# A transformer block on one core: the VectorE share of the softmax exponential as two summed terms instead of six, with more of it on VectorE and K projected without a trip through DRAM

## The chip, the cores and the metric

One of the eight cores of a Trainium2 chip runs the whole kernel. The core has five engines that work at the same time and wait for each other by semaphores: TensorE (PE: matmuls, and PEld: its weight loads), VectorE (DVE), ScalarE (ACT), GpSimd (POOL) and SyncE (SP), which here issues nearly all DMA transfers. Matmuls write to PSUM, eight banks of 512 fp32 values on each of 128 partitions; the other engines read them from there. SBUF is the large on-chip memory, DRAM is outside the core.

The metric is the device time of one execution in microseconds (us), the median of several runs. A profile is one further execution; its span is a little shorter than the device time.

## What is computed

A block with adaptive layer norm: attention with 32 heads of 20 dimensions over 2048 tokens, then a gated feed-forward part. Cut to what matters:

```python
# A_x [1, 2048, 640], A_wqkv [640, 1920], A_wo [640, 640]
# B_w_gate, B_w_up [640, 1536], B_w_down [1536, 640], c [1, 640], w_mod [640, 3840]
mod = (silu(c) @ w_mod).reshape(1, 6, 1, 640)
sa, ca, ga, sb, cb, gb = mod[:, 0], ..., mod[:, 5]

h = layernorm(x) * (1 + ca) + sa
q, k, v = split_heads(h @ wqkv)                  # 32 heads, Dh = 20
scores = einsum('bhqd,bhkd->bhqk', q, k) * Dh ** -0.5
p = softmax(scores)                              # 32 x 2048 x 2048 exponentials
x = x + ga * (merge_heads(einsum('bhqk,bhkd->bhqd', p, v)) @ wo)

h = layernorm(x) * (1 + cb) + sb
x = x + gb * (((h @ w_gate) * (h @ w_up)) @ w_down)   # B_x is not used
```

The exponentials are the largest elementwise part: 134 million of them.

## The kernel before

The program is written by a small scheduler in Python. Tasks carry an engine, a rough duration, a priority and dependencies; the scheduler runs them through a model of the engines once, and the order that comes out on each engine is what the chip executes. [...]

**Chunks, items, units, quads.** Queries are cut into five chunks. A chunk has eight items (four heads each), and an item is cut into units: one unit is a 128 x 512 tile of scores of one head. A unit goes either to ScalarE or, in fours called quads, to VectorE. `QUADS` says how many quads each item of each chunk has.

```python
CHUNKS = [(0, 512), (512, 512), (1024, 512), (1536, 256), (1792, 256)]
QUADS = [(1, 2, 2, 3, 2, 3, 2, 3), 3, 3, (1, 1, 2, 1, 1, 1, 1, 1), (1, 1, 1, 1, 1, 0, 0, 0)]
SHIFTS = (0, 18, 34, 56, 77, 105)
NB0, NSS = 3, 2        # buffers for VectorE's first and for its further terms
NPS = 4                # slots of exponentials, in each of two rings
K_DIRECT = (0, 1)
```

**Exponential on ScalarE** (L1214): groups of three and two units by turns, from PSUM to bf16 in SBUF.

```python
        def fexp(e, nu=nu, b0=b0, cellp=cellp, g=g):
            return e.activation(PPs[g % 2][:, cellp["p"], 0:nu * 512],
                                ps[:, b0:b0 + nu, :].rearrange("p b c -> p (b c)"), AFT.Exp, scale=ESCALE)
```

**Exponential on VectorE.** Q is scaled so that a score, plus a bias, written as a 16-bit integer is the bit pattern of a bf16 number near the exponential: the upper bits are the exponent, the lower seven a straight line in place of 2^f. This is one instruction a unit (L1238). To bend the straight lines to the curve, five more copies of the quad are made with other offsets (L1252), and all six terms are summed.

```python
            def fp1(e, st_=st_, x=x, cell=cell):
                return e.tensor_scalar(DB0[:, st_["slot"], x * 512:(x + 1) * 512], bank(cell["b"]), EBIAS, 0.0,
                                       op0=ALU.add, op1=ALU.max)
        ...
        for jj in range(1, NSH):
            def fsh(e, st_=st_, cell=cell, jj=jj):
                return e.tensor_scalar(DSS[:, cell["s"], :], DB0[:, st_["slot"], :], float(SHIFTS[jj]), None, op0=ALU.add)
            tsx = Task("dve", 575.0, fsh, list(st_["p1"]), prio=2.5 + .001 * qi,
                       name=f"SH.{qi}.{jj}")
            tsx.acq = [(sSS, "s", 1)]
```

**The sum costs no instruction of VectorE**: TensorE multiplies every term with V and accumulates in PSUM. A VectorE unit thus has six value matmuls where a ScalarE unit has one (L1596, four heads side by side, 32 columns of the array each). V carries a column of ones, so the softmax denominator comes out of the same sums.

```python
            ems.append(lambda e, i=i, kt=kt, stt=stt, stp=stp: e.matmul(
                ps[32 * s:32 * s + mc, BPV, 0:u.n],
                Vf[:, (kt * H + 4 * u.j + s) * VW:(kt * H + 4 * u.j + s) * VW + mc],
                srcf()[:, i * u.n:(i + 1) * u.n], tile_position=(0, 32 * s), start=stt, stop=stp,
                skip_group_check=True))
```

After an item's last value matmul VectorE transposes, divides and transposes back (L1305 to L1313). Items go through one PSUM bank, one after the other.

**Projections.** A score matmul reads K and Q of a head at partitions 32 s. `kq_round` ("direct", L862) projects four heads of 20 columns to 32-row places. `packed_round` (L914) projects 128 columns with no gaps, in fewer rounds, and the rows go to DRAM scratch and come back to their places:

```python
        # packed_round, K
        pcs = [(0, w, lambda: KS[656 * tc + r0:656 * tc + r0 + w, :])]
        ...
        kt_ready[(j, tc)] = [dma("sp", 32 * 1024, lambda e, j=j, s=s: e.dma_start(
            KT[32 * s:32 * s + 32, j, tc * 512:(tc + 1) * 512],
            KS[656 * tc + 80 * j + DH * s:656 * tc + 80 * j + DH * s + 32, :]),
            dps, prio=1.4, dur=450.0) for s in range(4)]
```

Here K of the first item's heads comes directly in the first two token blocks, Q of the first two items in the first block; all else is packed. An eviction of a projection (`evac`) can be taken over by ScalarE early in the kernel.

**The feed-forward part** of a chunk (`suffix`) is spread by gates over the next chunk's exponentials; that of the last chunk stands alone at the end.

The softmax here doesn't subtract the row's maximum and nothing guards it: scores larger than these inputs give would overflow.

## Time and profile before

| | |
|---|---|
| device time, median of 3 runs | 869.92 us (869.12 to 872.37) |
| span of the profile | 865.9 us |
| ScalarE, exponentials (L1214) | 691 instructions, 788.3 us busy |
| TensorE, scores (L1180) | 2560 matmuls, 295.2 us busy |
| TensorE, values with ScalarE's units (L1596, PP) | 2184 matmuls, 171.9 us busy |
| TensorE, values with VectorE's terms (L1596, DSS and DB) | 2256 matmuls, 183.8 us busy |
| VectorE, first term (L1238) | 320 instructions, 217.2 us busy |
| VectorE, shifted terms (L1252) | 400 instructions, 265.9 us busy |
| transposes of an item's sums (L1305) | first 63.2 us, last 830.4 us |

"Busy" is the time in which at least one instruction of the group runs on its engine; the mean of one instruction can be longer than the step from one to the next, since neighbours overlap. A line such as `L1214` is the line of the kernel that wrote the instruction, `out<-in` names the tiles. Where the profile says `<-PE ps_all L1180 9.7`, the engine was idle for 9.7 us before instructions of that group until that line of PE released them.

### The profile page before, as it was taken

To read this page: it belongs to the slowest core of one execution; us is meant where nothing else is said; L and a number is where in the kernel's file an instruction comes from. 1 tells how busy PE (TensorE), PEld (TensorE's weight loads), DVE (VectorE), ACT (ScalarE), POOL (GpSimd) and SP (SyncE) were. 2 spreads that over 40 slices of the span, in tenths; PEclk is the share of its full clock that TensorE was granted. 3 is DMA by queue.
4 is the path that set the end of the run, shared out by engine and by line. 5 is a ranking of instruction groups with operands and counts; after the bars stand their busy time and mean duration, and the time that the engine had idled before them with its cause. 6 is when DMAs were issued, how large, how long until landed. Compare 5 with 4: busy or idle time off the path is not lost.

```text
span 865.9 us, 30616 instructions
## 1 busy us (share of the span) xinstructions
PE 829.4 (96%) x13568; PEld 327.5 (38%) x13568; DVE 713.1 (82%) x1338; ACT 802.5 (93%) x718; POOL 32.0 (4%) x65
## 2 busy tenths in 40 slices
PE   8899999999999999999999999999999999999998
PEld 4433333322233322233333322223445444455577
DVE  7865888796999999999889999999779877775463
ACT  4698999999999999899999999999999999999931
POOL 2300000000001000000000100000001100000000
PEclk9997999999999999999999999999999999999999
DMA  9163331122510125110301011110310036203640
GB/s 300 38 216 94 92 86 37 29 71 76 156 29 23 33 55 146 43 24 6 66 10 44 5 36 44 44 36 2 67 50 7 21 75 139 59 21 82 136 88 18
DMA packets 118459, 56.37 MB, mean 65 GB/s; under 512 B 84439, under 2 KB 118327, under 8 KB 118327
## 3 DMA queue, kind: packets, MB, share of 16 engines
q1 hardware_dynamic: 117399, 53.26, 24.2%
q8 instruction: 107, 1.75, 0.9%
q10 hardware_dynamic: 928, 1.15, 0.4%
q14 instruction: 25, 0.20, 0.1%
HBM read 42.93 MB, written 9.16 MB: 60 GB/s over the span
## 4 chain that ended last, share of the span: by engine, by line
PE 44%; ACT 34%; DVE 15%; issue 3%; DMA 2%; POOL 1%; SPq 1%; DVEq 0%; ACTq 0%
ACT PP L1214 34%; PE ps_all L747 16%; PE ps_all L1596 13%; PE ps_all L1180 12%; DVE DB L1238 4%; DVE DSS L1252 3%; PE ps_all L914 2%; DVE st L802 1%; DMA k_rows<-KPA 1%; DVE st L1400 1%; DVE xck L1390 1%; DVE OT L1305 1%; DVE xn L1407 1%; PE ps_all L829 1%; DMA stg<-in_B_w_gate_dram 1%
## 5 line engine op out<-in xcount | busy, mean ns | idle before, releaser
L1214 ACT ACTIVATE PP<-ps_all 128x1536 bf16<-128x1536 f32 (+1 forms) x691 | 788.3, 1279 | 13.5 <-PE ps_all L1180 9.7
L1180 PE MATMUL ps_all<-QT,KT 32*128 32x512 bf16 (+1 forms) x2560 | 295.2, 341 | 14.5 <-ACT PP L1214 11.5
L1252 DVE TENSOR_SCALAR DSS<-DB 128x2048 int16<-128x2048 int16 x400 | 265.9, 683 | 20.0 <-PE ps_all L1596 17.7
L1238 DVE TENSOR_SCALAR DB<-ps_all 128x512 int16<-128x512 f32 x320 | 217.2, 682 | 38.7 <-PE ps_all L1180 37.0
L1180 PEld LDWEIGHTS ps_all<-QT,KT 32*128 32x128 bf16 x2560 | 77.2, 91 | 256.6 <-ACT PP L1214 185.7
L1596 PE MATMUL ps_all<-PP,Vf 128*32 128x512 bf16 (+3 forms) x2184 | 171.9, 344 | 1.5 <-DVE OT L1305 1.5
L1596 PE MATMUL ps_all<-DSS,Vf 128*32 128x512 bf16 (+2 forms) x1880 | 151.7, 351 | 0.0
L747 PE MATMUL ps_all<-h2T,stg 128*32 128x512 bf16 x1440 | 109.7, 381 | 2.8 <-DVE DB L1238 1.7
L1596 PEld LDWEIGHTS ps_all<-PP,Vf 128*32 128x32 bf16 (+1 forms) x2184 | 48.3, 94 | 95.3 <-issue 84.9
L1596 PEld LDWEIGHTS ps_all<-DSS,Vf 128*32 128x32 bf16 (+1 forms) x1880 | 47.8, 96 | 36.1 <-issue 16.0
L747 PE MATMUL ps_all<-wd,hprod 128*32 128x320 bf16 x1152 | 55.2, 300 | 0.4 <-DVE DB L1238 0.3
L747 PEld LDWEIGHTS ps_all<-h2T,stg 128*32 128x32 bf16 x1440 | 34.8, 96 | 35.1 <-issue 9.4
L1465 DVE CAST gsb<-ps_all 128x512 bf16<-128x512 f32 (+1 forms) x48 | 29.5, 615 | 10.8 <-PE ps_all L747 10.6
L747 PEld LDWEIGHTS ps_all<-wd,hprod 128*32 128x32 bf16 x1152 | 29.2, 96 | 14.9 <-issue 4.8
L747 PE MATMUL ps_all<-wV,hT 128*32 128x320 bf16 x640 | 32.9, 300 | 1.9 <-DVE DB L1238 0.8
L1403 POOL TENSOR_SCALAR sd<-mv 128x1 f32<-128x1 f32 x14 | 7.0, 499 | 739.7 <-DVE mv L1402 739.7
L747 PE MATMUL ps_all<-wo,Ocp 128*32 128x320 bf16 x640 | 31.9, 300 | 0.4 <-DVE xck L1390 0.3
L1596 PE MATMUL ps_all<-DB,Vf 128*32 128x512 bf16 (+2 forms) x376 | 32.1, 349 | 0.0
L1305 DVE STREAM_TRANSPOSE OT<-ps_all 128x512 f32<-128x512 f32 (+1 forms) x40 | 24.2, 605 | 8.8 <-PE ps_all L1596 8.6
L914 PE MATMUL ps_all<-hT,wk 128*32 128x512 bf16 x380 | 29.9, 381 | 0.4 <-DVE Vf L994 0.4
L914 PE MATMUL ps_all<-hT,wq 128*32 128x512 bf16 x375 | 29.0, 394 | 0.9 <-DVE Vf L994 0.3
L1476 DVE TENSOR_TENSOR hprod<-ps_all,gsb 128x512 bf16<-128x512 f32 x36 | 24.5, 681 | 5.3 <-PE ps_all L747 5.3
(107 smaller groups left out, 486.6 us busy)
## 6 DMA issues: line engine op xcount, KB each, us to landing
stg<-in_B_w_gate_dram SPq DMA_DIRECT2D x50, 160.0 KB
stg<-in_B_w_up_dram SPq DMA_DIRECT2D x50, 160.0 KB
KT<-k_rows SPq DMA_DIRECT2D x120, 32.0 KB
QT<-q_rows SPq DMA_DIRECT2D x22, 128.0 KB
wm<-in_w_mod_dram SPq DMA_DIRECT2D x3, 800.0 KB
k_rows<-KPA SPq DMA_DIRECT2D x18, 128.0 KB
x<-in_A_x_dram SPq DMA_DIRECT2D x7, 320.0 KB
xck<-in_A_x_dram SPq DMA_DIRECT2D x3, 640.0 KB
```

The lines of the kernel that those rows point to most:

```text
L747: return lambda e, b: e.matmul(ps[32 * x:32 * x + 32, b, 0:n], lhs()[:, 32 * x:32 * x + 32], rhs(), tile_position=(0, 32 * x), start=st, s ...
L802: bns.append(dve(393, lambda e, t=t, i=i, hf=hf: e.bn_stats(st[:, i, 6 * hf:6 * hf + 6], x0[:, t, 320 * hf:320 * hf + 320]), [d_x[tc][i // ...
L829: f = lambda e, b, i=i, k=k: e.transpose(bankh(b)[:, i * 128:(i + 1) * 128], xn[:, s2, i, k * 128:(k + 1) * 128], ident[:])
L914: f = [lambda e, b_, k=k, x=x: e.matmul(ps[x:x + min(32, w - x), b_, :], wx[:, k, r0 + x:r0 + min(x + 32, w)], hT[tc][:, k, :], tile_posit ...
L1180: ems.append(lambda e, i=i, kt=kt: e.matmul(dstf()[:, i * u.n:(i + 1) * u.n], KT[32 * u.s:32 * u.s + 32, u.j, kt * 128:(kt + 1) * 128], QT ...
L1214: return e.activation(PPs[g % 2][:, cellp["p"], 0:nu * 512], ps[:, b0:b0 + nu, :].rearrange("p b c -> p (b c)"), AFT.Exp, scale=ESCALE)
L1238: return e.tensor_scalar(DB0[:, st_["slot"], x * 512:(x + 1) * 512], bank(cell["b"]), EBIAS, 0.0, op0=ALU.add, op1=ALU.max)
L1252: return e.tensor_scalar(DSS[:, cell["s"], :], DB0[:, st_["slot"], :], float(SHIFTS[jj]), None, op0=ALU.add)
L1305: t1 = Task("dve", n * 1.1 + 70, lambda e: e.transpose(OT[:, 0:n], ps[:, BPV, 0:n]), [], prio=0.0, name=f"T1.{it}")
L1465: f = lambda e: e.tensor_copy(gsb[:, gs, 0:n], ps[:, r.b["b"], 0:n])
L1476: f = lambda e: e.tensor_tensor(hprod[:, fc, 0:n], ps[:, r.b["b"], 0:n], gsb[:, gs, 0:n], ALU.mult)
L1596: ems.append(lambda e, i=i, kt=kt, stt=stt, stp=stp: e.matmul(ps[32 * s:32 * s + mc, BPV, 0:u.n], Vf[:, (kt * H + 4 * u.j + s) * VW:(kt * ...
```

## The change

On VectorE the exponential becomes a parabola in the mantissa. Read the 16-bit pattern as 2^e (1+f). Masking out the mantissa and setting the exponent of one half gives (1+f)/2; its product with the pattern itself is 2^e (1+f)^2 / 2. The second term is the pattern with the mantissa cleared but for one bit, 2^e (1 + 2/128). Their sum, 2^e ((1+f)^2 / 2 + 1.016), is close to 1.5 times 2^(e+f), and the constant factor goes into the bias. So a quad has two terms in place of six, made by three instructions in place of five: mask and exponent in the form of the shift, and one product of two tensors. The value matmuls of a VectorE unit fall from six to two. What is freed is used to move more units from ScalarE: 92 quads in place of 80.

K of all heads and Q of the first token block are projected directly. K never goes to DRAM; more projection rounds are run for it.

Further constants of the scheduler (leads, gates, priorities) are set anew.

```diff
-QUADS = [(1, 2, 2, 3, 2, 3, 2, 3), 3, 3, (1, 1, 2, 1, 1, 1, 1, 1), (1, 1, 1, 1, 1, 0, 0, 0)]
-SHIFTS = (0, 18, 34, 56, 77, 105)
-D_LEAD = 0.35
-NB0, NSS = 3, 2
+QUADS = [(3, 2, 3, 3, 3, 3, 4, 3), 3, (3, 3, 3, 3, 3, 3, 4, 3), (1, 2, 1, 2, 1, 2, 0, 2), 1]
+D_LEAD = 0.377
+NB0, NSS = 2, 3
 NPS = 4
+TS_4X, TT_2X = 600.0, 1145.0
 ... (gates, leads)
-K_DIRECT = (0, 1)
-K_LEAD = 0.4
+K_DIRECT = (0, 1, 2, 3)
+Q_DIRECT = 8
+K_ALL = (0, 1, 2, 3)
+KD_LEAD = 0.593
 ...
-SHIFT_GAIN = 3.046480226123085
+QUAD_GAIN = 0.597233983857778
+NTERM = 2
 ...
-    late.append((.95, 2560, lambda p, g: kq_round("Q", 1, 0, p, g)))
-    for b in range(4):
+    for j in range(1, Q_DIRECT):
+        late.append((j - .05, 2560, lambda p, g, j=j: kq_round("Q", j, 0, p, g)))
+    for b in range(4 if Q_DIRECT < NSET else 0):
 ...
     for tc in range(4):
-        for b in range(nblk(tc)):
+        for j in range(1, NSET if tc in K_ALL else 0):
+            late.append((j + tc / 4 - KD_LEAD, 2560, lambda p, g, j=j, tc=tc: kq_round("K", j, tc, p, g)))
+        for b in range(0 if tc in K_ALL else nblk(tc)):
 ...
-        for jj in range(1, NSH):
-            def fsh(e, st_=st_, cell=cell, jj=jj):
-                return e.tensor_scalar(DSS[:, cell["s"], :], DB0[:, st_["slot"], :], float(SHIFTS[jj]), None, op0=ALU.add)
+        def fm(e, st_=st_):
+            return e.tensor_scalar(DSS[:, st_["ss"][0], :], DB0[:, st_["slot"], :], 0x7F, 0x3F00, op0=ALU.bitwise_and,
+                                   op1=ALU.bitwise_or)
+
+        def fx(e, st_=st_):
+            d = DSS[:, st_["ss"][0], :].bitcast(BF16)
+            return e.tensor_tensor(d, DB0[:, st_["slot"], :].bitcast(BF16), d, ALU.mult)
+
+        def fe(e, st_=st_):
+            return e.tensor_scalar(DSS[:, st_["ss"][1], :], DB0[:, st_["slot"], :], 0x7F80, 2, op0=ALU.bitwise_and,
+                                   op1=ALU.bitwise_or)
+        tm = term(fm, list(st_["p1"]), TS_4X, "M", slot=0)
+        term(fx, [tm], TT_2X, "X", src=0, last=True)
+        term(fe, list(st_["p1"]), TS_4X, "EX", slot=1, src=1, last=True)
```

## The prediction

> **What bounds the kernel now.** I read the page's busy line first, then ScalarE's timeline and waits, then a table by stage, then the groups by shape, then a few microseconds of VectorE and TensorE. The busy line:

> ```profile
> PE 829.4 (96%) x13568; PEld 327.5 (38%) x13568; DVE 713.1 (82%) x1338; ACT 802.5 (93%) x718; POOL 32.0 (4%) x65
> ```

> Two engines look full. Which one sets the end is told by who waits for whom. ScalarE's timeline shows its first exponential at 17.28 us and the last one ending at 829.00 us, and between long runs without a gap:

> ```profile
> 339.73 25.32 ACT L1214 ACTIVATE PP<-ps_all 128x1536 bf16<-128x1536 f32 x22
> 367.41 2.37 ACT L1214 ACTIVATE PP<-ps_all 128x1536 bf16<-128x1536 f32 x2 [2.36 <-PE ps_all L1596]
> 370.11 50.57 ACT L1214 ACTIVATE PP<-ps_all 128x1536 bf16<-128x1536 f32 x44 [0.34 <-PE ps_all L1180]
> ```

> The columns are start, length, instruction, count and, in brackets, the idle time before. 44 ACTIVATEs (22 pairs of three and two units; a unit is one 512-wide score tile) take 50.57 us: 2.30 us for five units, 0.46 us a unit. In the view of waits ScalarE waits for TensorE only briefly, while TensorE's weight loads wait mostly for ScalarE to free score banks:

> ```profile
> PEld ps_all L1180 <- ACT PP L1214: 185.7, 471, 1.4
> ...
> ACT PP L1214 <- PE ps_all L1180: 9.7, 14, 2.6
> ```

> The table by stage (I cut at the first exponential, 120 us, the four chunk changes and the last exponential; columns are window, its length, busy time and count of PE, PEld, DVE, ACT, POOL, granted clock, DMA share, GB/s):

> ```profile
> 17.30:120.00 102.70, 95.78 (x1408) 36.09 (x1404) 75.10 (x157) 88.70 (x81) 9.79 (x22) 0.95 0.42 115
> 120.00:238.00 118.00, 113.94 (x1500) 34.94 (x1492) 98.31 (x166) 117.90 (x105) 0.00 (x0) 1.00 0.27 74
> 238.00:429.00 191.00, 185.37 (x2499) 59.58 (x2491) 181.79 (x319) 187.70 (x166) 5.09 (x8) 1.00 0.20 48
> 429.00:620.00 191.00, 185.34 (x2541) 60.05 (x2542) 178.09 (x310) 190.22 (x168) 4.38 (x8) 1.00 0.13 32
> 620.00:724.00 104.00, 99.57 (x2138) 48.66 (x2130) 84.69 (x164) 103.51 (x92) 5.93 (x8) 1.00 0.18 45
> 724.00:829.00 105.00, 103.08 (x2334) 54.05 (x2330) 64.61 (x132) 104.89 (x92) 1.58 (x4) 1.00 0.41 89
> 829.00:866.00 37.00, 32.60 (x1020) 27.27 (x1020) 17.54 (x45) 4.47 (x12) 1.23 (x2) 1.00 0.12 33
> ```

> ScalarE's busy time from 17.3 to 829 us sums to 792.9 of 811.7 us, so it idles 18.8 us, of which 14.0 us lie before 120 us and 3.3 us in the second chunk. So three pieces make the span: 17.3 us until the first exponential, 811.7 us of ScalarE with little idle, 37 us of last gated block. In the middle only fewer ScalarE units, or less of those 18.8 us, can shorten it. VectorE is at 95% and 93% in the third and fourth windows: it is what keeps more units from moving to it.

> [...]

> ```profile
> L1252 DVE TENSOR_SCALAR DSS<-DB 128x2048 int16<-128x2048 int16 x400 | 265.9, 683 | 20.0 <-PE ps_all L1596 17.7
> L1238 DVE TENSOR_SCALAR DB<-ps_all 128x512 int16<-128x512 f32 x320 | 217.2, 682 | 38.7 <-PE ps_all L1180 37.0
> L1162 DVE TENSOR_TENSOR wo<-wo,gab 128x640 bf16<-128x640 bf16 x5 | 2.3, 467 | 0.0
> L1310 DVE TENSOR_TENSOR OTn<-OT,invT 128x512 bf16<-128x512 f32 x24 | 16.4, 682 | 0.2
> ```

> [...] 640 bf16 elements take less time (467 ns) than 512 with an fp32 input (682 ns). No run yet shows 2048 in tensor_tensor. [...] no trace here has an AND/OR. [...]

> **Part by part.** One full instruction behind another starts 0.60 us later on VectorE (timeline, starts 281.08, 281.68, 282.28 us):

> ```profile
> 281.08 0.68 DVE L1238 TENSOR_SCALAR DB<-ps_all 128x512 int16<-128x512 f32 x1
> 281.68 0.68 DVE L1252 TENSOR_SCALAR DSS<-DB 128x2048 int16<-128x2048 int16 x1
> 282.28 0.69 DVE L1238 TENSOR_SCALAR DB<-ps_all 128x512 int16<-128x512 f32 x1
> ```

> and four concurrent 512-wide value matmuls start 0.22 us after the four before them (482.56 and 482.78 us):

> ```profile
> 482.56 0.39 PE L1596 MATMUL ps_all<-DB,Vf 128*32 128x512 bf16 x4
> 482.78 0.39 PE L1596 MATMUL ps_all<-DSS,Vf 128*32 128x512 bf16 x4
> ```

> Units: 3 x 8 x 64 + 2 x 8 x 32 = 2048. A quad moves four to VectorE. Before 2048 - 320 = 1728 on ScalarE, after 2048 - 368 = 1680, so 48 fewer. At 0.46 us that is **-22.1 us** on the bounding engine (chunk by chunk 24, 0, 4, 8 and 12 units: -11.0, 0, -1.8, -3.7, -5.5).

> VectorE, per quad: before 4 reads of PSUM + 5 shifts = 9 x 0.60 = 5.40 us, 80 quads 432 us. After 4 reads + mask + exponent = 6 x 0.60, [...] The order of instructions shows 49 projection evictions on it after, 38 before (+6.6 us), and three layer-norm evictions fewer (about 0.5 us each). In all about +10 us: flat. But it shifts: in the second chunk 24 quads fall from 129.6 to 113.8 us, so its 95% falls to about 87%. In the first chunk 18 quads (97 us) become 24 (114 us), and with the evictions 173 us of 221 us (first two windows) become some 195 us of about 210 us, 93%. Full, not over.

> TensorE: the summed terms go from 6 x 320 = 1920 to 2 x 368 = 736 unit matmuls, by fours 480 to 184 times 0.22 us, -65 us; ScalarE's units -48, -2.6 us. Projections of Q and K go from 835 to 1100 matmuls, +265, +66 fours, +14.6 us. Net -53 us, in an engine that ScalarE makes wait: no direct gain. Scores are unchanged at 2560 matmuls.

> ScalarE also takes evictions in the head: by the order, hT 9 instead of 6 (0.78 us each), KT 4 instead of 2 and KPA 0 instead of 1 (0.59 us each): **+2.9 us**, partly inside idle time.

> DRAM scratch: 24 writes of K rows and 120 reads into KT go, and the packed rounds of the first Q. The chain of waits has such a transfer from 50.5 to 68 us, but ScalarE runs 13 ACTIVATEs from 50.13 to 65.17 us: hidden there. What it may give is a part of the 14.0 us idle before 120 us. On the other side stand the extra projection rounds, in a stretch where PE is busy 93%. I take **-5 us** of idle in all (an estimate, from 18.8 us present), of which the second chunk's 3.3 us are the easiest.

> First exponential: the same three projections and the same transposes go ahead of it, 0. End: the last item has a quad now and had none, so its last value matmuls may wait for VectorE: **+1 us**, a guess; the 37 us themselves run the same matmuls.

> Sum: 865.9 - 22.1 + 2.9 - 5 + 1 = 842.7 us of span. The device time before is 869.92 us for a span of 865.9 us, 4.0 us more: about 846 us.

> **Rivals.** (a) ScalarE has no idle time left after the change: 17.3 + 336 x 2.30 + 7.6 (head evictions) + 37 + 4.0 gives 839 us. For it: TensorE has 53 us less to do. Against it: the early idle time comes from transposes and projections that must be done first. (b) VectorE becomes the bound in the first chunk: at 93% by my count, value matmuls of a quad then come late, the eight slots of exponentials fill and ScalarE stops. Were the load 5% over full, ScalarE would lose about 10 us of the 210: 853 to 857 us. (c) [...] Slower by far; only the missing measurement of a bit operation speaks for it. (d) PE had been the true limit and 53 us come off: below 825 us; the gapless ScalarE rows speak against it.

> **Range and chances.** The floor of (a) and the middle of (b) bound the range, 838 to 857 us. 2% faster is 852.5 us, above the sum by 6 us; it takes most of (b) to miss it. Faster 0.81, same 0.15; slower, nearly (c) alone, 0.04.

> **What would show it.** Right: 672 ACTIVATEs of exponentials still at 2.30 us a pair, in runs of 20 and more; mask and exponent near 683 ns[...]; ScalarE idle between first and last exponential under 18 us; PE busy well below 96%; the tail near 37 us. Wrong: ScalarE waiting for scores that wait for VectorE's quads before 230 us, a bit operation of 2 us or more, a first exponential later than 18 us, or a tail of 40 us.

## The result and the profile after

The changed kernel takes **857.71 us** (853.04 to 857.92, 4 executions) beside 869.99 us: ratio 0.9848, 95% interval 0.9819 to 0.9877. Measured again later, six executions beside their own runs of the kernel before: 851.4 us, ratio 0.9821 (0.9787 to 0.9855). It is faster by 1.5 to 1.8%; 846 us had been predicted, in a range of 838 to 857 us: the first median lies 0.7 us above that range, the second inside it. A ratio is always the time over that of the kernel before, measured beside it.

The page of the changed kernel, its busy line and four groups (count, then busy us and mean ns of one):

```profile
PE 798.6 (93%) x12393; PEld 308.9 (36%) x12393; DVE 718.1 (84%) x1270; ACT 780.8 (91%) x703; POOL 31.2 (4%) x65
...
L1220 ACT ACTIVATE PP<-ps_all 128x1536 bf16<-128x1536 f32 (+1 forms) x672 | 763.8, 1319 | 23.6 <-PE ps_all L1186 22.9
...
L1277 DVE TENSOR_TENSOR DSS<-DB,DSS 128x2048 bf16<-128x2048 bf16 x92 | 111.1, 1208 | 0.1
...
L1272 DVE TENSOR_SCALAR DSS<-DB 128x2048 int16<-128x2048 int16 x92 | 62.5, 679 | 1.3
L1280 DVE TENSOR_SCALAR DSS<-DB 128x2048 int16<-128x2048 int16 x92 | 62.7, 681 | 1.0 <-PE ps_all L1616 1.0
```

The work is what it was meant to be: 672 exponentials on ScalarE, the product at 1208 ns, mask and exponent at 680 ns, as fast as the shifts they replace (683 ns). ScalarE's timeline shows where the gain leaks (start, length, count, idle before and what ended it):

```profile
41.43 5.57 ACT L1220 ACTIVATE PP<-ps_all 128x1024 bf16<-128x1024 f32 x5 [3.63 <-PE ps_all L1186]
49.73 3.07 ACT L838 ACTIVATE hT<-ps_all,mcol 128x512 bf16<-128x512 bf16 x4 [2.73 <-PE ps_all L832]
59.44 103.54 ACT L1220 ACTIVATE PP<-ps_all 128x1536 bf16<-128x1536 f32 x91 [6.64 <-PE ps_all L1186]
166.93 37.31 ACT L1220 ACTIVATE PP<-ps_all 128x1024 bf16<-128x1024 f32 x33 [3.95 <-PE ps_all L1186]
...
221.12 367.01 ACT L1220 ACTIVATE PP<-ps_all 128x1536 bf16<-128x1536 f32 x324 [1.65 <-PE ps_all L1186]
...
785.77 34.22 ACT L1220 ACTIVATE PP<-ps_all 128x1536 bf16<-128x1536 f32 x30 [1.59 <-PE ps_all L1186]
```

In the middle 324 ACTIVATEs run without a gap, 162 pairs at 2.266 us. The longest such row of the kernel before is this:

```profile
89.66 197.77 ACT L1214 ACTIVATE PP<-ps_all 128x1536 bf16<-128x1536 f32 x174 [1.48 <-PE ps_all L1180]
```

That is 87 pairs at 2.273 us, nearly the same pace. The prediction's 2.30 us came in part from reading a shorter row: a row's length counts its last ACTIVATE in full and the others only from start to start, and neighbours overlap (the two of a pair take 1.49 and 1.07 us in the mean of the kernel before, 2.56 us together). Ahead of the rows of L1220 shown above ScalarE waits for scores. The view of waits:

```profile
PEld ps_all L1186 <- ACT PP L1220: 198.5, 495, 1.2
...
ACT PP L1220 <- PE ps_all L1186: 22.9, 15, 6.6
```

TensorE's weight loads still mostly wait for ScalarE, but ScalarE's waits for scores are 22.9 us where they were 9.7 us. Three windows of the table by stage:

```profile
17.30:120.00 102.70, 95.60 (x1371) 36.59 (x1368) 85.99 (x167) 84.97 (x80) 10.10 (x23) 0.97 0.26 70
120.00:230.00 110.00, 104.20 (x1338) 33.08 (x1339) 96.14 (x152) 103.06 (x91) 0.00 (x0) 0.97 0.06 17
230.00:420.00 190.00, 178.44 (x2326) 56.51 (x2322) 174.86 (x286) 189.95 (x169) 5.01 (x8) 1.00 0.26 67
```

In the first two windows VectorE (third pair of columns) is at 182 of 212.7 us, 86%, and not the bound. ScalarE (fourth) idles 17.7 us in the first and 6.9 us in the second, where the first two windows of the kernel before had 14.0 and 0.1 us.

The span as a sum along ScalarE, from its timeline (idle: the gaps between its rows, first to last exponential); the last column is a later profile of the same changed kernel, used below:

| us | before | changed | changed, again |
|---|---|---|---|
| until the first exponential | 17.3 | 17.9 | 17.6 |
| exponentials | 789.7 | 764.5 | 764.3 |
| other ScalarE work between | 4.7 | 7.7 | 7.5 |
| idle between | 17.3 | 29.9 | 24.4 |
| after the last exponential | 36.9 | 35.8 | 35.8 |
| span | 865.9 | 855.8 | 849.5 |

25.2 us of exponentials are saved and 12.6 us come back as idle time, with 3.0 us of added evictions. The question for the experiments was what makes the 12.6 us.

### The profile page after: what moved, and what is told of

It is laid out like the page before. It is cut to its first block, busy times and chain, and to the rows that moved or that the text cites. A ratio compares the mean times of both kernels' runs of the same rounds, so it can differ in the third digit from the quotient of the medians. Undisturbed runs are those within 1.5% of the kernel's fastest.

```text
span 855.8 us, 28189 instructions
## 1 busy us (share of the span) xinstructions
PE 798.6 (93%) x12393; PEld 308.9 (36%) x12393; DVE 718.1 (84%) x1270; ACT 780.8 (91%) x703; POOL 31.2 (4%) x65
## 3 DMA queue, kind: packets, MB, share of 16 engines
q1 hardware_dynamic: 106998, 45.14, 21.2%
## 4 chain that ended last, share of the span: by engine, by line
ACT 41%; PE 35%; issue 12%; DVE 11%; POOL 0%; ACTq 0%; DVEq 0%
ACT PP L1220 41%; PE ps_all L750 13%; PE ps_all L1186 10%; PE ps_all L1616 7%; DVE DB L1244 3%; PE ps_all L865 2%; DVE st L805 1%; PE ps_all L917 1%; DVE DSS L1272 1%; DVE DSS L1277 1%; DVE OT L1325 1%; DVE hT L840 0%; DVE xn L816 0%; DVE OTn L1330 0%; DVE OcT L1333 0%
## 5 line engine op out<-in xcount | busy, mean ns | idle before, releaser
L1220 ACT ACTIVATE PP<-ps_all 128x1536 bf16<-128x1536 f32 (+1 forms) x672 | 763.8, 1319 | 23.6 <-PE ps_all L1186 22.9
L1186 PE MATMUL ps_all<-QT,KT 32*128 32x512 bf16 (+1 forms) x2560 | 310.6, 342 | 31.8 <-ACT PP L1220 24.3
L1244 DVE TENSOR_SCALAR DB<-ps_all 128x512 int16<-128x512 f32 x368 | 247.3, 682 | 60.2 <-PE ps_all L1186 59.2
L1186 PEld LDWEIGHTS ps_all<-QT,KT 32*128 32x128 bf16 x2560 | 81.5, 91 | 269.8 <-ACT PP L1220 198.5
L1616 PE MATMUL ps_all<-PP,Vf 128*32 128x512 bf16 (+1 forms) x2116 | 167.8, 345 | 0.2
L1277 DVE TENSOR_TENSOR DSS<-DB,DSS 128x2048 bf16<-128x2048 bf16 x92 | 111.1, 1208 | 0.1
L1616 PEld LDWEIGHTS ps_all<-PP,Vf 128*32 128x32 bf16 (+1 forms) x2116 | 47.8, 94 | 91.8 <-issue 83.2
L1616 PE MATMUL ps_all<-DSS,Vf 128*32 128x512 bf16 (+2 forms) x888 | 76.2, 353 | 0.2
L1272 DVE TENSOR_SCALAR DSS<-DB 128x2048 int16<-128x2048 int16 x92 | 62.5, 679 | 1.3
L1280 DVE TENSOR_SCALAR DSS<-DB 128x2048 int16<-128x2048 int16 x92 | 62.7, 681 | 1.0 <-PE ps_all L1616 1.0
L865 PE MATMUL ps_all<-hT,wk 128*32 128x512 bf16 x640 | 46.8, 386 | 2.3 <-ACT hT L838 0.9
L1325 DVE STREAM_TRANSPOSE OT<-ps_all 128x512 f32<-128x512 f32 (+1 forms) x40 | 24.1, 604 | 10.2 <-PE ps_all L1616 10.1
L1616 PEld LDWEIGHTS ps_all<-DSS,Vf 128*32 128x32 bf16 (+1 forms) x888 | 23.8, 96 | 19.7 <-issue 7.6
```

The source lines that it names most:

```text
L865: f = [lambda e, b, k=k, s=s: e.matmul(ps[32 * s:32 * s + 32, b, :], wx[:, k, w0 + DH * s:w0 + DH * s + 32], hT[tc][:, k, :], tile_positio ...
L1186: ems.append(lambda e, i=i, kt=kt: e.matmul(dstf()[:, i * u.n:(i + 1) * u.n], KT[32 * u.s:32 * u.s + 32, u.j, kt * 128:(kt + 1) * 128], QT ...
L1220: return e.activation(PPs[g % 2][:, cellp["p"], 0:nu * 512], ps[:, b0:b0 + nu, :].rearrange("p b c -> p (b c)"), AFT.Exp, scale=ESCALE)
L1272: return e.tensor_scalar(DSS[:, st_["ss"][0], :], DB0[:, st_["slot"], :], 0x7F, 0x3F00, op0=ALU.bitwise_and, op1=ALU.bitwise_or)
L1277: return e.tensor_tensor(d, DB0[:, st_["slot"], :].bitcast(BF16), d, ALU.mult)
L1280: return e.tensor_scalar(DSS[:, st_["ss"][1], :], DB0[:, st_["slot"], :], 0x7F80, 2, op0=ALU.bitwise_and, op1=ALU.bitwise_or)
```

## The experiments

Candidates: the three quads in the first item; the direct projections; TensorE's granted clock, which the trace shows at 0.5 in more places than before; or the claim itself that ScalarE sets the end. This table gathers what the runs' traces show; the idle columns are ScalarE's gaps in us by stretch of the span, "half" is the time at granted clock 0.5 between about 22 us and the end:

| run | time, us | to 70 | 70-120 | 120-240 | 240-725 | later | half, us |
|---|---|---|---|---|---|---|---|
| before | 869.99 | 8.3 | 5.4 | 0 | 3.7 | 0 | 10.2 |
| changed | 857.71 | 17.4 | 0 | 6.9 | 1.9 | 3.7 | 27.3 |
| terms only | 873.39 | 8.0 | 15.8 | 0 | 0.2 | 0.8 | 27.3 |
| direct only | 876.96 | 7.5 | 0.9 | 8.2 | 1.7 | 0.4 | 3.4 |
| K through DRAM | 860.38 | 15.0 | 10.0 | 0 | 11.7 | 0.5 | 61.4 |
| clock held up | 863.17 | 18.9 | 0 | 8.7 | 3.6 | 1.2 | 6.8 |
| item 0, one quad | 848.32 | 10.2 | 1.0 | 4.5 | 3.3 | 0.3 | 6.8 |
| Q earlier | 859.67 | 17.7 | 0 | 3.1 | 6.7 | 2.9 | 44.4 |
| direct, set again | 845.98 | 7.2 | 0 | 4.7 | 4.0 | 0 | 17.1 |
| DRAM, set again | 848.16 | 8.3 | 5.7 | 2.4 | 5.0 | 0.7 | 23.9 |
| same 92 quads | 861.24 | 10.2 | 1.4 | 11.9 | 4.5 | 1.1 | 23.9 |
| quads later | 857.08 | 13.2 | 8.0 | 6.8 | 1.9 | 0.5 | 20.5 |
| changed, again | 851.4 | 17.9 | 0 | 4.0 | 1.9 | 0.5 | 10.2 |

One caution holds for all but two of them: every new constant lets the scheduler write a new order everywhere, so a time carries all its side effects. The stretches are read with more trust than the sums.

**The terms alone.** The new exponential with the old quads, the old paths of K and Q and the old leads and gates (but two first buffers and three others, as in the change).

```diff
-QUADS = [(3, 2, 3, 3, 3, 3, 4, 3), 3, (3, 3, 3, 3, 3, 3, 4, 3), (1, 2, 1, 2, 1, 2, 0, 2), 1]
-K_DIRECT, Q_DIRECT, K_ALL = (0, 1, 2, 3), 8, (0, 1, 2, 3)
+QUADS = [(1, 2, 2, 3, 2, 3, 2, 3), 3, 3, (1, 1, 2, 1, 1, 1, 1, 1), (1, 1, 1, 1, 1, 0, 0, 0)]
+K_DIRECT, Q_DIRECT, K_ALL = (0, 1), 2, ()
 (leads, gates and caps as before the change)
```

> Only the new exponential (two terms, three VectorE instructions a quad) with the 80 quads of before, K packed through DRAM and all leads and gates of before. Theory (ScalarE sets the end; TensorE and VectorE work only matter through the waits they cause): 1728 units stay on ScalarE, so its exponentials stay near 785 us, the idle time between first and last exponential near 19 us, and the time near 866 us (ratio 0.99 to 1.00), although TensorE loses some 70 us and VectorE some 50 us of work. Rival (TensorE at 96% was a bound of its own): the time falls with TensorE's work, to 850 us or less.

873.39 us, ratio 1.0029 (1.0007 to 1.0051): not faster at all. VectorE's busy time falls from 713.1 to 659.6 us and 1386 matmuls are gone, and none of it reaches the end, because ScalarE's exponentials take 787.5 us as before. That TensorE bounds the kernel is out. The loss against the expected 866 us is mostly one wait, in ScalarE's timeline of this run:

```profile
85.80 2.36 ACT L1220 ACTIVATE PP<-ps_all 128x1536 bf16<-128x1536 f32 x2 [0.32 <-PE ps_all L1186]
98.01 2.37 ACT L1220 ACTIVATE PP<-ps_all 128x1536 bf16<-128x1536 f32 x2 [9.84 <-PE ps_all L1186]
```

The scores at the end of that wait stood waiting for Q, which in this run still comes back from DRAM for most heads (TensorE's timeline):

```profile
97.56 0.70 PE L1186 MATMUL ps_all<-QT,KT 32*128 32x512 bf16 x7 [3.95 <-DMA QT<-q_rows]
```

The page's clock row shows a dent in slices 4 and 5 of its 40 (the two lower digits), which lie between about 65 and 109 us:

```profile
PEclk9997799999999999999999999999999999999999
```

The two halved stretches in it are 74.1 to 84.3 and 98.0 to 108.2 us. During the wait itself the clock is at 1.00, as a window over it shows (clock third from the end):

```profile
88.20:98.00 9.80, 5.68 (x45) 2.12 (x36) 1.91 (x5) 0.00 (x0) 0.00 (x0) 1.00 0.50 119
```

So the late Q makes this wait, and not the clock.

**The direct projections alone**, in the kernel before (80 quads, six terms; the hunks of `K_ALL` and `Q_DIRECT` applied, `KD_LEAD = 0.593`).

> Only the projection part: six terms and 80 quads as before, but K of all heads and Q of the first block direct, constants of before otherwise. Theory (the added projection rounds, 265 matmuls, sit in the first chunk ahead of scores that ScalarE waits for, and the DRAM trip they replace was hidden): ScalarE idles more in the first 240 us, time 874 to 882 us (ratio 1.005 to 1.014). Rival (the DRAM trip was the wait of the head): less idle time before 120 us, 860 to 866 us.

876.96 us, ratio 1.0094 (1.0052 to 1.0137): a cost, as the theory had it, but only partly where it had it. Idle time before 240 us grows from 13.7 to 16.6 us: the wait before 120 us shrinks from 13.7 to 8.4 us, so the packed path did cost something there (in the kernel before no gap of ScalarE between 70 and 120 us is traced to a transfer, and 3.1 of the 5.4 us lie at half clock, 77.8 to 88.0 us), and 8.2 us appear between 120 and 240 us. Another 3.7 us is a longer tail (40.6 us) and 1.1 us a later start.

**K through DRAM in the changed kernel**, and most of the first block's Q with it, as before the change.

```diff
-K_DIRECT, Q_DIRECT, K_ALL = (0, 1, 2, 3), 8, (0, 1, 2, 3)
+K_DIRECT, Q_DIRECT, K_ALL = (0, 1), 2, ()
```

> The changed kernel with its 92 quads, but K packed through DRAM and only two Q projections direct, as before the change. Theory (direct rounds cost ScalarE idle time in the first chunk, 3.95 us at 163 us and a part of the 13 us between 36 and 60 us): 849 to 853 us (ratio 0.976 to 0.981). Rival 1 (the early idle time comes from item 0's three quads on VectorE): unchanged, 855 to 859 us. Rival 2 (the direct path is the gain): above 860 us.

860.38 us (856.65 to 865.51), ratio 0.9871 (0.9841 to 0.9900): my theory missed, and the median falls to rival 2, by 0.4 us. The profile is that of the slowest execution. In it the wait at 163 us is gone, but 10.0 us stand at 70 to 120 us and 11.7 us after 240 us, with 61 us at half clock; 4.11 of the 10.0 us are again a wait for scores whose Q is late from DRAM. The execution of this kernel at a mean clock of 0.980 took 856.65 us, the changed one at 0.982 857.6 us: at like clock the paths are level, as far as two executions tell.

**The clock, with the order kept.** The changed kernel with the same order on each engine, and the score matmuls of 56 groups (the ranges below) doubled.

```diff
     end = sc.run()
+    for each PE task "S<g>" (and the VectorE scores behind it) with g in
+            11..15, 126..137, 139..150, 462..475, 628..640:
+        task.emits = task.emits + task.emits
```

> The changed kernel with every instruction in the same order; only the score matmuls of 57 groups, placed just ahead of the stretches where the granted clock fell to 0.5 (around 45, 200, 215, 585 and 775 us), are issued twice (the second writes the same numbers over the first). Theory ([...]the halved clock then starves ScalarE): the clock stays at 1.0 in the four late stretches, ScalarE's idle time there (7.5 us) falls under 2 us, time 849 to 853 us. Rival (the halved clock only accompanies a wait that has another cause): the idle time stays or grows by the added matmuls, 857 to 862 us.

863.17 us, ratio 0.9919 (0.9898 to 0.9940): longer. The clock half of the theory, an estimate that thin stretches of TensorE's work bring the halving, agrees: behind every doubled stretch except the first, the clock stayed at 1.00 (27.3 us at half fell to 6.8 us). The time half did not: after 725 us the idle time fell from 3.7 to 1.2 us, but elsewhere each doubled group cost ScalarE up to 0.9 us of its own. Another execution of the changed kernel (the last run below) escaped three of the four late halvings with nothing doubled, so one profile is weak evidence that more matmuls keep the clock up; the mean clocks point the same way, 0.990 to 0.996 in four executions here, 0.982 to 0.994 in ten of the changed kernel. What the clock is worth this run can't tell.

**One quad in the first item.**

```diff
-QUADS = [(3, 2, 3, 3, 3, 3, 4, 3), 3, ...
+QUADS = [(1, 2, 3, 3, 3, 3, 4, 3), 3, ...
```

> The changed kernel with one quad in the first item in place of three (90 quads, 8 units more on ScalarE). Theory (in the head VectorE's quads compete with the projection evictions for VectorE and for the two shared score banks, and so delay the last block of K): ScalarE's idle time before 70 us falls from 17.4 us to 10 us or less, its exponentials grow by 3.7 us, and the time falls to 850 to 854 us. Rival (the head waits for the added direct projections whatever the quads): idle before 70 us stays at 15 us or more and the time rises by the 3.7 us, to 860 to 863 us.

848.32 us (848.25 to 849.23), ratio **0.9764** (0.9749 to 0.9780), with eight units *more* on ScalarE. Idle before 70 us is 10.2 us. ScalarE's timeline of this run:

```profile
42.05 6.88 ACT L1220 ACTIVATE PP<-ps_all 128x1024 bf16<-128x1024 f32 x6 [2.95 <-PE ps_all L1186]
...
53.74 26.19 ACT L1220 ACTIVATE PP<-ps_all 128x1024 bf16<-128x1024 f32 x23 [2.89 <-PE ps_all L1186]
...
162.94 77.41 ACT L1220 ACTIVATE PP<-ps_all 128x1536 bf16<-128x1536 f32 x68 [4.46 <-PE ps_all L1186]
```

Full work begins at 53.74 us in place of 59.44 us. What stood in the way in the changed kernel shows in its timeline of all engines, 46 to 50 us:

```profile
46.95 0.39 PE L1186 MATMUL ps_all<-QT,KT 32*128 32x512 bf16 x1
47.35 0.68 DVE L1272 TENSOR_SCALAR DSS<-DB 128x2048 int16<-128x2048 int16 x1
...
47.49 0.39 PE L1186 MATMUL ps_all<-QT,KT 32*128 32x512 bf16 x1 [0.16 <-DVE DB L1244]
47.95 1.88 DVE L1244 TENSOR_SCALAR DB<-ps_all 128x512 int16<-128x512 f32 x3
...
48.69 0.38 PE L1186 MATMUL ps_all<-QT,KT 32*128 32x512 bf16 x1 [0.81 <-DVE DB L1244]
...
49.29 0.40 PE L832 MATMUL ps_all<-ident,xn 128*128 128x128 bf16 x4 [0.21 <-DVE DB L1244]
```

VectorE's scores go one by one, each waiting for VectorE to empty a bank, and the transposes of the last token block, which K and the next scores of ScalarE need, come only after them. From 47.00 us ScalarE has nothing but evictions until 59.44 us.

Not all of the 9.4 us between 857.71 and 848.32 us is the head's. All four executions here ran at a mean clock of 0.994 to 0.996; the changed kernel at 0.994, in the last run below, took 849.64 us. Beside that run's profile the head saves 7.7 us of idle time, and the exponentials of the eight units cost 4.5 us (768.8 us against 764.3 us). So most of the 9.4 us goes with the clock. That this order keeps the clock higher is suggested by its four executions, no more.

**Q earlier.**

```diff
-        late.append((j - .05, 2560, lambda p, g, j=j: kq_round("Q", j, 0, p, g)))
+        late.append((j - .15, 2560, lambda p, g, j=j: kq_round("Q", j, 0, p, g)))
```

> The changed kernel with the direct Q rounds asked for 0.15 of an item before their item and not 0.05. Theory (at 163 us ScalarE waits 3.95 us because the next item's Q and K rounds stand behind a run of V rounds): that wait is gone and the time falls by 3 to 4 us, to 853 to 855 us. Rival (the order is only pushed about, and the wait turns up at another item): idle time between 120 and 240 us stays near 7 us, time 856 to 860 us.

859.67 us (853.03 to 861.85): the wait at 163 us falls from 3.95 to 0.94 us as expected, and the time doesn't follow; 44 us run at half clock, 23.9 us of it in one piece around 470 us. Its one execution at a mean clock of 0.986 took 853.03 us, where the changed kernel took 857.19 and 857.64 us at 0.986: there the 4 us are seen, but in one execution. Inconclusive on that wait; its place in the changed kernel's timeline is this:

```profile
162.03 1.25 PE L865 MATMUL ps_all<-hT,wk 128*32 128x512 bf16 x20
...
163.11 0.85 PE L750 MATMUL ps_all<-wV,hT 128*32 128x320 bf16 x20
...
164.22 1.25 PE L865 MATMUL ps_all<-hT,wq 128*32 128x512 bf16 x20
165.30 1.25 PE L865 MATMUL ps_all<-hT,wk 128*32 128x512 bf16 x20
...
166.49 0.61 PE L1186 MATMUL ps_all<-QT,KT 32*128 32x512 bf16 x6
```

K, V, Q and K again stand in a row ahead of the scores that ScalarE waits for. A wait of 2.7 to 8.3 us stands near 160 us in seven of the nine traces with direct projections (about 1 us in the other two, this run and the direct one set again); those of the kernel before and of the runs with K through DRAM have none there. In the direct projections alone it is ended by a value matmul and not by scores, so the row above isn't the cause in all seven.

**Leads, gates and quads set again**, for both paths of K. The edit shown is that of the direct one; the one through DRAM has 91 quads too, none of them in the first item, and leads and gates of its own.

```diff
-QUADS = [(3, 2, 3, 3, 3, 3, 4, 3), 3, (3, 3, 3, 3, 3, 3, 4, 3), (1, 2, 1, 2, 1, 2, 0, 2), 1]
+QUADS = [(1, 2, 2, 3, 3, 3, 4, 3), (3, 3, 3, 3, 4, 4, 3, 2), (3, 3, 3, 3, 3, 3, 4, 3),
+         (1, 2, 1, 2, 1, 2, 0, 2), (1, 1, 1, 2, 1, 1, 1, 1)]          # direct: 91 quads
+V_L, FILL_MIN, GATE_F[2], LN2P, HT_L, LATEQ_A, LATEQ_F = 0.297, 4800.0, 0.914, 1.643, 0.03, 1, 0.855
```

> The changed kernel with its leads, gates and quads set again (21, 25, 25, 11 and 9 quads, one in the first item; K and Q direct). Theory (what the change lost is idle time of ScalarE in the first 240 us, so an order without it shows the gain): idle time between first and last exponential 12 to 18 us, time 843 to 849 us (ratio 0.968 to 0.976). Rival (the gain is lost to a limit of TensorE, VectorE or the clock that no order mends): 855 us or more.

> The same for the path of K through DRAM: two-term exponential, 91 quads (none in the first item), K packed as before the change, with leads and gates set again. Theory (the DRAM trip was hidden and the direct rounds cost TensorE and VectorE work in the first chunk): at least as fast as the direct version set again, 838 to 848 us. Rival (what made the packed K slow beside the two-term exponential at 860 us is the path itself, its late arrival and the halved clock that goes with it): 855 us or more.

845.98 us (843.9 to 851.12), ratio **0.9744** (0.9701 to 0.9787), and 848.16 us (846.1 to 850.3), ratio 0.9760 (0.9737 to 0.9783). Both beat the changed kernel's first measurement, and by less its later one of 851.4 us; the intervals of the two overlap, so that the path through DRAM is at least as fast isn't shown, and it ended 0.2 us above its range. Each path keeps a wait of its own: through DRAM 4.74 us at 89 us, again for scores with a late Q, direct some 2 us near 164 us. So the path of K is worth little by itself, and with the first item lightened (one quad here, none in the other) and the constants set again, the gain I had summed is there.

**The same 92 quads, two of them moved** out of the first item.

```diff
-QUADS = [(3, 2, 3, 3, 3, 3, 4, 3), 3, ...
+QUADS = [(1, 3, 3, 3, 3, 3, 4, 4), 3, ...
```

> The changed kernel with all its 92 quads, but one in the first item and the two others in items 1 and 7 of the same chunk: ScalarE has the same 1680 units. Theory (it is where the quads stand, in the first item, that costs): idle before 70 us near 10 us as with one quad and 90 in all, time 845 to 851 us. Rival (90 quads instead of 92 relieved VectorE in the first chunk as a whole): idle time comes back later in the chunk, between 120 and 240 us, time 855 to 860 us.

The head does as the theory says, 10.2 us of idle, the same as with 90 quads; the time does as the rival says, 861.24 us, ratio 0.9905 (0.9878 to 0.9932). 8.25 us of waiting begin at 158.6 us, where V, K and Q rounds again stand ahead of the scores, and the tail is 39.3 us. VectorE is busy 93.2 us of the 110 us from 120 us on, 85%, so a full VectorE, as the rival put it, doesn't make that wait. So the head's cost belongs to the quads of the first item, and not every order that mends the head is a better order.

**The quads later.**

```diff
-            due.append(max(18.0, a0 + na * (x / len(dus) - D_LEAD)))
+            due.append(max(30.0, a0 + na * (x / len(dus) - D_LEAD)))
```

> The changed kernel with three quads in the first item, but the earliest of all quads not due before the 30th unit of ScalarE instead of the 18th. Theory (VectorE's quads collide with the projections of the last K block while they run before about 50 us; later they do not): idle before 70 us falls from 17.4 to 12 us or less, time 848 to 853 us. Rival (three quads in the first item hold its end, and so the single bank of value sums, whenever they start): idle time moves to 60 to 120 us, time 855 us or more.

857.08 us, ratio 0.9864 (0.9843 to 0.9885), idle before 70 us 13.2 us, and 8.0 us more until 78 us. The wait has moved, and its releaser is another, in ScalarE's timeline of this run:

```profile
66.46 3.45 ACT L1220 ACTIVATE PP<-ps_all 128x1024 bf16<-128x1024 f32 x3 [0.25 <-PE ps_all L1186]
78.00 87.73 ACT L1220 ACTIVATE PP<-ps_all 128x1536 bf16<-128x1536 f32 x77 [8.09 <-PE ps_all L1616]
```

L1616 is a value matmul: ScalarE's slots are full. In the trace the last terms of the first item's quads go through TensorE at 75.75 us, VectorE starts to transpose the item's sums at 76.80 us, and the next value matmuls, at 77.56 us, end the wait: the first item can't end before its three quads do. So, beside the 10.2 us with one quad, three quads there cost 7 us (17.4 us) or 11 us (21.2 us until 78 us) of idle time at the two starts tried; the rival was right on that.

**The changed kernel again**, nothing edited.

> The changed kernel itself, to see one instruction order under different granted clocks. Theory (each halved window starves ScalarE for a part of it): among its executions the time falls as the mean granted clock rises, some 5 us for 0.01 of mean clock, as 857.6 us at 0.982 and 853.0 us at 0.990 suggest. Rival (the clock is only a companion): the times do not line up with the clock.

All ten executions of this one order, time and mean granted clock: 849.64 us at 0.994; 851.22, 851.33 and 851.46 at 0.992; 853.04 at 0.990; 857.19 and 857.64 at 0.986; 857.59, 857.83 and 857.92 at 0.982. They line up, if not on a straight line. The profile at 0.992 beside the first one: same instructions, same head (17.9 us idle), same wait at 163 us, and from there on this:

```profile
59.64 103.55 ACT L1220 ACTIVATE PP<-ps_all 128x1536 bf16<-128x1536 f32 x91 [7.11 <-PE ps_all L1186]
167.15 418.14 ACT L1220 ACTIVATE PP<-ps_all 128x1024 bf16<-128x1024 f32 x369 [3.95 <-PE ps_all L1186]
...
774.54 4.84 ACT L1220 ACTIVATE PP<-ps_all 128x1536 bf16<-128x1536 f32 x4 [0.22 <-PE ps_all L1186]
```

The gaps at 204 to 221 us are gone and those at 777 to 786 us nearly. 17.1 us less at half clock go with 6.3 us less of span, in this pair of profiles about 0.37 us for each us at half clock. The table of windows of the first profile, cut finely, shows how a halving comes about (length, PE busy and matmuls, PEld, DVE, ACT, POOL, clock, DMA share, GB/s):

```profile
774.90:778.30 3.40, 2.45 (x24) 0.98 (x27) 2.63 (x6) 2.85 (x4) 1.20 (x2) 0.76 0.89 199
778.30:781.70 3.40, 3.40 (x46) 1.43 (x42) 1.25 (x4) 2.16 (x3) 0.00 (x0) 0.50 1.22 238
781.70:785.10 3.40, 3.40 (x62) 1.73 (x52) 2.17 (x6) 2.20 (x2) 0.00 (x0) 0.50 0.25 45
```

A stretch with few matmuls (24 in 3.40 us), then half clock with TensorE busy all the time, and ScalarE busy only 2.2 of 3.4 us, since its scores come late. That the few matmuls bring the halving is an estimate from this order of events.

## Why the prediction was right or wrong

- **ScalarE sets the end: right.** Shown by the terms alone: 1386 matmuls and 53 us of VectorE's busy time less, and no gain.
- **-22.1 us for 48 units: right**, 25.2 us measured. A unit took 0.457 us on the mean before and 0.455 us after (789.7 us for 1728 units, 764.5 us for 1680), which makes 21.9 us for the 48 units and 3.3 us for the rest. **+2.9 us of evictions: right**, 3.0 us.
- **VectorE's durations: right.** The duration that the prediction took for the product stood on no trace or run; 1208 ns is the measured one. The next instruction starts 1.13 us after it (the changed kernel's timeline, 284.82 and 285.95 us), and with that VectorE's count comes out as predicted: 6 x 0.60 + 1.13 = 4.73 us a quad, 435 us for 92. Mask and exponent take 679 and 681 ns, so rival (c), bit operations far slower than the shift, is out. Rival (b), VectorE full in the first chunk, is out as put: 86% there, not 93%. But its sign, scores of ScalarE that stand behind VectorE's quads, did come, in the first item. The second chunk came out at 92% and not at 87%.
- **First exponential and tail: right within 1 us** (+0.6 and -1.1 us, against 0 and +1).
- **-5 us of idle: this step failed.** It is +12.6 us in the first profile (+7.1 us in the second). That is 17.6 us from what was taken, more than the whole miss of the span (855.8 against 842.7 us); the other terms came out 4.5 us better than summed. The step set the saving of the DRAM trip and of a relieved TensorE against the added rounds and took 5 us as what is left. A saving of that size is there: the 5.4 us of gaps between 70 and 120 us are gone. Three things outweigh it:
  - The head, +9.1 us: three quads in the first item in place of one. 7.2 us of it are shown by two runs: one quad brings the idle time to 10.2 us with 90 quads and with 92. A third, the later start, doesn't lower the idle time. The other 1.9 us aren't explained. I had counted VectorE's load of the first chunk as a share, not what its quads hold up in the first item.
  - The wait at 163 us, 3.95 us. It goes with the direct projections, whose rounds the prediction had set against the saving without a figure for what they make ScalarE wait. That the row of K, V and Q rounds makes it is read from the trace, not shown: the run that shortened it was faster only in the one execution at like clock.
  - The halved clock. With less work on TensorE (798.6 us busy in place of 829.4 us) some stretches become thin, and the clock fell after them, as shown for 777 us (24 matmuls in 3.40 us, then 0.50). In the first profile the later gaps, from 204 us on, are 8.5 us, most of them in or next to halved stretches, where the kernel before had 3.7 us after 120 us. At a clock of 0.992 to 0.994 the changed kernel takes 850 to 851 us. So of the 11.7 us between 846 and 857.7 us some 6 to 8 us go with the clock, and what makes one execution halve more often than another stays open.
- **+4.0 us from span to device time: too much.** In every execution whose span is on record the device time is 1.8 to 1.9 us above the span of the same execution; the rest of the 4.0 us lay between two executions of the kernel before.
- **Rival (a)**, no idle time left, 839 us: no version came nearer than 843.9 us, one execution of the direct one set again.
- **The chances.** 0.81 stood on "faster by over 2%", 0.15 on what came. The sum lay only 6 us inside the limit, and its largest estimated term was nearly of that size.

## What to carry to other kernels

When an engine that isn't the bound loses work, the gain can be nil until work is moved off the engine that is: here the new exponential by itself made the time 0.3% longer, and the gain came only in runs with the units moved. Sum idle time by stretch and ask of each new placement what it holds up there: a share of load over a whole chunk hides that the first item has no slack. And after relief of TensorE look at its granted clock before trusting a small difference between two orders: here one order took 849.64 us at a mean clock of 0.994 and 857.92 us at 0.982.
